# Attention with normalised q and k, then a squared-ReLU feed-forward: fewer rows of rounding beside the attention, q's transposes moved, loads in three groups

## The chip, the cores and the metric

The kernel runs on one core of a Trainium2 chip. The metric is the device time of one execution in microseconds, as the median of several runs. One further execution was recorded by the hardware profiler; all lines of profile below come from it. The engines of a core are TensorE (PE; its weight loads are listed as PEld), VectorE (DVE), ScalarE (ACT), GpSimd (POOL) and SyncE (SP), which here only issues DMAs. Each works through its own queue in order and waits on semaphores for the others.

## The reference

Eight batches of twelve heads, 448 tokens, head size 64; then a feed-forward layer over 3584 tokens with 768 inputs and 2048 hidden units.

```python
def rmsnorm(x, g):
    rms = np.sqrt(np.mean(x * x, axis=-1, keepdims=True) + 1e-06)
    return x / rms * g
q_n, k_n = rmsnorm(q, g_q), rmsnorm(k, g_k)
scores = np.matmul(q_n, k_n.transpose(0, 1, 3, 2)) / np.sqrt(64)
attn = softmax(scores)
x = np.matmul(attn, v).transpose(0, 2, 1, 3).reshape(3584, 768)
h = np.maximum(x @ w_in, 0.0)
out = (h * h) @ w_out
```

q, k, v and the gains are float32; the weights w_in and w_out come as float64 and are brought to float32 in the kernel, word by word. That is "the rounding".

## The kernel before

All is float32. Two heads make a pair (128 rows of q, k and v transposed), six pairs a batch, two batches a span, four spans. The kernel's order is written out by hand: Python generators yield between steps, and a loop puts the steps of two of them beside each other.

The first attention (`attention_alone`, pairs 0 to 11, NAT = 12) stands alone, with the rounding of w_in beside it. Then comes L1 of span 0 (`first_product(work, 0)`), the first product with w_in, with the rest of the rounding beside it; then, for each next span, its attention beside the second product of the span before, and so on. The products use seven block products for eight (A11, S2, S1, S3, A12, A22, S4), and the combined weight blocks are written to DRAM (`w1s`, `w2s`) by the rounding and read back as `sw`.

One pair i of the first attention takes four steps, each ended by a yield:

- Step 1: scores (i,0) and (i,1) on TensorE (L812), their exponentials on ScalarE (L816); k's four transposes for pair i+1 (L787) into a PSUM bank, copied to `qkT` by ScalarE (L789); the last eight products of the values of pair i-1 (L875); VectorE adds up probabilities (L829); the square and the sums for the norm of pair i+2 (L727 to L729).
- Step 2: q's four transposes for pair i+1 (L787) into the same bank as k's, copied with the gain by ScalarE (L791); v of the next pair is loaded; `roots(i + 2)` takes the inverse root through a logarithm and an exponential on ScalarE (L738, L739), three small operations on VectorE (L740 to L742), and GpSimd multiplies q by it (L743). Pairs 1 and 2 do this in `normalise_in_turn` instead, with a power on GpSimd (L336) and the product on VectorE (L339).
- Step 3: scores (i,2) and (i,3); the totals of pair i-1 (L900), of two parts for odd pairs and three for even ones; the first eight products of the values of pair i; then `finish(i - 1)` on VectorE: two transposes and a reciprocal of the totals (L918 to L920) and the product L924, which reads the values' bank.
- Step 4: VectorE adds up further (L829) and combines x (L934 to L939).

PSUM banks: scores use two buffers of two banks (`ps_s`); the values of even pairs lie in bank "o", those of odd pairs in bank "n", the totals in "t"; the transposes of steps 1 and 2 in bank "m".

The rounding (`prepare`, one row of weights after another, 32 rows: 16 of w_in, 16 of w_out) takes four ticks a row. A row costs ScalarE an absolute value (L594) and a copy of the low words (L611), VectorE a clamp (L608), a shift (L613) and a mask (L618), and one sum: for rows before EARLY/4 in two halves on GpSimd (L580), for later ones on VectorE (L584). Each two rows make four combinations on GpSimd (L588) and one write of 1344 KB to DRAM (L603). The row's words, 768 KB, are loaded four rows ahead (L545, L548). `weights(upto)` runs the ticks up to a number that grows with the step u: in the attention up to EARLY, in L1 of span 0 from EARLY to ALL = 140 over its 56 units.

L1 has HF = 8 groups of seven units. A unit u multiplies one weight block (192 KB) by three chunks (L1100). The block's buffer is one of five, so block u+4 is issued in unit u (L677) once unit u-1 is through. SyncE's queue holds all of these in order: the blocks, the words of the rounding, its writes, which wait for GpSimd, and, at unit 40, v for pair 12 (L713, L715) and q and k for pair 14 (L696) of the next attention.

Of the kernel before, what the change touches and what calls it, by code (L numbers as in the profile page):

```python
# [10 lines left out]
F32 = mybir.dt.float32  # L11
U32 = mybir.dt.uint32
AF = mybir.ActivationFunctionType
# [298 lines left out]
def load_q(nc, qk, q, i):  # L312

    _, H, S, D = q.shape
    b, h0 = divmod(2 * i, H)
    nc.sync.dma_start(places_of(qk, i, 0)[:S // 4, 0].rearrange("p (h e) -> p h e", h=2),
                      q[b, h0:h0 + 2].rearrange("h (p j) d -> p h (j d)", j=4))


def load_k(nc, qk, k, i):  # L320

    _, H, S, D = k.shape
    b, h0 = divmod(2 * i, H)
    dst = places_of(qk, i, 0)[:S // 4, 1].rearrange("p (j h d) -> p j h d", j=4, h=2)
    for h in range(2):
        nc.sync.dma_start(dst[:, :, h], k[b, h0 + h].rearrange("(p j) d -> p j d", j=4))
# [18 lines left out]
def chunk_of(pt, s, j, n):  # L345

    return pt.rearrange("d (j p) -> d j p", j=n)[:, j] if s else pt.rearrange("d (p j) -> d j p", j=n)[:, j]
# [45 lines left out]
def attention_then_ffn_bounded(  # L393
# [35 lines left out]
    nc = tc.nc  # L429

    B, H, S, D = q.shape
    NT, DM = out.shape
    DFF = w_in.shape[1]
    P = 128
# [3 lines left out]
    NFC = DFF // P  # L438
# [9 lines left out]
    NAT = 2 * NPAIR  # L448
# [12 lines left out]
    ps_o = ctx.enter_context(tc.tile_pool(name="ps_o", bufs=1, space=bass.MemoryType.PSUM))  # L461
# [3 lines left out]
    def bank(name, n=None):  # L465

        turn[0] += n is None
        return ps_m.tile([P, S], F32, tag="mn"[turn[0] % 2 if n is None else n], name=name)

    qk, qkT, ident, mhalf, gains, rstd0, _ = held  # L470
# [20 lines left out]
    HW = HC * P  # L491
    WORDS, BLOCKS, EXPS = 7, 2, 4

    EARLY, ALL = 4 * 12, 4 * (2 * NFC + 3)
    assert DM == NW and BLOCKS * 8 * HW + EXPS * NW + 2 * NW <= 3 * HF * S and 2 * NW <= 4 * S and HF % 4 == 0


# [156 lines left out]
    N1 = HF * 7  # L654
# [25 lines left out]

    pts = {}
    vs, probs, pavs, tots, normed, rstds = {}, {}, {}, {}, {}, {0: rstd0}
    places, halves, rests = [], [], {}
    sums = {"out": [dram.tile([2 * S // 32, 32], F32, name=f"factors{n}") for n in range(2)]}

    def load(i):
        if i < NAT:
            load_q(nc, qk, q, i)
            load_k(nc, qk, k, i)
            return  # L690

        b, h0 = i // NPAIR, 2 * (i % NPAIR)
        for s, src in enumerate((q, k)):
            dst = by_squares(i, 0)[:, s]
            for n in range(4):
                nc.sync.dma_start(dst[n * 32:(n + 1) * 32],  # L696
                                  src[b, h0 + n // 2, :, n % 2 * 32:n % 2 * 32 + 32]
                                  .rearrange("(g t) e -> t g e", t=32))

    def by_squares(i, work):  # L700
        n = i % 2 * 4 + 2 * work
        flat = qk[:, n:n + 2].rearrange("p n e -> p (n e)")[:, 0:2 * S]
        return flat.rearrange("p (s g e) -> p s g e", s=2, e=32)
# [78 lines left out]

    def transpose(i, s, n):

        pt = bank("pt", n)
        for j in range(NJ):
            nc.tensor.transpose(chunk_of(pt, s, j, NJ), normed[i][s][:, j * P:(j + 1) * P], ident[:SP, :SP])  # L787
        if s:
            nc.scalar.copy(qkT[:, i % 2, s], pt)  # L789
        else:  # L790
            nc.scalar.activation(qkT[:, i % 2, s], pt, AF.Copy, scale=gains[:, 0:1])  # L791

    def scores(i, c):

# [73 lines left out]
    def values(i, chunks=range(NJ)):  # L868
        if 0 in chunks:
            pavs[i] = ps_o.tile([P, S], F32, tag="o", name="pav") if i >= NAT or i % 2 == 0 else bank("pav", 1)  # L870
        if i >= NAT:
            return later_values(i)
        for c in chunks:
            for h in range(2):
                nc.tensor.matmul(pavs[i][h * D:(h + 1) * D, :], vs[i][:SP, h, c, :], probs[i, c][:, h, :],  # L875
                                 start=(c == 0), stop=(c == NJ - 1))
# [12 lines left out]
    def added(i):  # L889

        return 3 if i % 2 and i + 1 < NAT else 2
# [16 lines left out]
    def finish(i):  # L908

        b, hp = divmod(i, NPAIR)  # L910
        x = factors = xT[:, b % 2, hp]
        if i < NAT:
            pav = pavs.pop(i)


            turned, factors = sums["turned"], sums["factors"]
            few = small.tile([P, S // 32], F32, tag="few", name="few", bufs=1)
            nc.vector.transpose(turned, tots.pop(i))  # L918
            nc.vector.reciprocal(few, turned.rearrange("p (g r) -> p g r", r=32)[:, :, 0])
            nc.vector.transpose(factors.rearrange("p (g r) -> p g r", r=32),  # L920
                                few.rearrange("p g -> p g ()").to_broadcast([P, S // 32, 32]))
        else:
            pav = rests.pop(i)
        nc.vector.tensor_tensor(x, pav, factors, ALU.mult)  # L924
        del vs[i]
# [15 lines left out]
    def attention_alone():  # L941


        for i in range(NAT):
            more = i + 1 < NAT
            if 0 < i < NAT - 3:
                load(i + 3)
            scores(i, 0)
            scores(i, 1)
            if i == 0:  # L950

                transpose(1, 1, 1)
                scores(0, 2)
                scores(0, 3)
                transpose(1, 0, 0)
                add_up(0, 1)
                norm(2)
                load_v(1)
                values(0, (0, 1))
                load(3)  # L960
                yield
                continue
            if more:
                transpose(i + 1, 1, 0)
            values(i - 1, (2, 3))
            add_up(i, 1)
            if i + 2 < NAT:
                norm(i + 2)
            elif not more:
                norm(NAT)  # L970
            yield
            if more:
                transpose(i + 1, 0, 0)
            if more:
                load_v(i + 1)
            if i + 2 < NAT:
                roots(i + 2)
            yield
            scores(i, 2)
            scores(i, 3)  # L980
            total_of(i - 1)
            values(i, (0, 1))
            finish(i - 1)
            yield
            if added(i) == 3:
                add_up(i, 2)
            combine_x(i - 1)
            if NAT <= i + 3 < NAT + 2:
                load(i + 3)
            yield  # L990
        values(i, (2, 3))
        total_of(i)
        finish(i)
        combine_x(i)

# [486 lines left out]
    with tc.tile_pool(name="words", bufs=2) as spare["pool"]:  # L1482
        load(2)
        for _ in range(2):
            load_w(loaded[0])
            loaded[0] += 1
        norm(1)
        with tc.tile_pool(name="first", bufs=2, reuse_waits="tile") as work:

            free = [gT[:, f] for f in range(NFC) if f % HF < HF - 2]  # L1490
            places[:] = [g.rearrange("p (h q) -> p h q", h=2) for g in free[:2 * NJ]]
            sums[0], sums[1] = (g.rearrange("p (h q) -> p h q", h=2) for g in free[2 * NJ:2 * NJ + 2])
            sums["turned"], sums["factors"] = (g[:, 0:S] for g in free[2 * NJ + 2:2 * NJ + 4])
            sums["ones"] = work.tile([SP, D], F32, tag="ones", name="ones", bufs=1)
            nc.vector.memset(sums["ones"], 1.0)
            sums["rebias"] = work.tile([SP, 1], F32, tag="rebias", name="rebias", bufs=1)
            nc.vector.memset(sums["rebias"], -31.5 * math.log(2.0))
            for u, _ in enumerate(attention_alone()):

                weights(min(EARLY, 2 * u + 1, 4 + (EARLY - 4) * u // (4 * NAT - 7)))  # L1500
                if u == 4 * NAT - 9:
                    load_blocks(5)
        with tc.tile_pool(name="first_product", bufs=2, reuse_waits="tile") as work:
            for u, _ in enumerate(first_product(work, 0)):
                if u == 6:

                    left = ps_s.tile([P, 2, 512], F32, tag="s", name="bits")
                    banks["bits"] = left.rearrange("p a b -> p (a b)")[:, 0:NW].bitcast(U32)
                weights(min(ALL, EARLY + (ALL - EARLY) * (u - 1) // (N1 - 6)))
                if u == 5 * N1 // 7:  # L1510
                    load_v(NAT)
                    load(NAT + 2)
                if u == N1 - 5:
                    norm(NAT + 1)
                if u == N1 - 4:
                    transposes(NAT)
                    squares(NAT + 2)
# [124 lines left out]
```

## Time and profile before

| | us |
|---|---|
| runs | 1339.31, 1340.26, 1340.64 |
| median | 1340.26 |
| profiled execution | 1340.13 |
| its span | 1338.3 |
| first attention, in the span | 8.9 to 128.3 |
| L1 of span 0, in the span | 128.3 to 257.4 |
| TensorE busy | 1322.2 |

In the table of waits, "A <- B: us, times, longest" says that engine and line A waited for B. In a timeline a row has its start, its length, engine and line, what is written and read, the number of instructions, and in brackets the idle time before it and what ended it. One matrix product of float32 shows as two instructions of TensorE, so three products of a unit are six rows. In the table by stretches each engine has its busy time, and the last columns are the granted clock of TensorE, the busy share of the DMA engines and GB/s.

The groups of VectorE between 140 and 240 us, with busy time and mean length of one in ns, show what the rounding costs there:

```profile
L613 DVE TENSOR_SCALAR bits<-gC 128x768 uint32<-128x768 uint32 x18 | 17.2, 957 | 0.4
L608 DVE TENSOR_SCALAR gC<-gC 128x768 f32<-128x768 f32 x19 | 15.5, 817 | 1.0 <-ACT gC L594 1.0
L584 DVE CUSTOM_DVE_ANT_0 gC<-words,gC 128x1536 uint16<-128x1536 uint16 x10 | 11.0, 1097 | 0.0
L618 DVE SCALAR_TENSOR_TENSOR gC<-words,bits 128x768 uint32<-128x768 uint32 x9 | 8.6, 952 | 0.2
```

### The profile page before, as it was taken

The numbers are of one execution on the slowest core, as the hardware profiler recorded it, in microseconds if no ns is written. First come the engines' busy times: TensorE is split into PE (matmuls) and PEld (weight loads), VectorE is DVE, ScalarE is ACT, GpSimd is POOL, SyncE is SP. The second block draws the span as 40 slices with busy tenths as digits, with TensorE's granted clock in tenths as the row PEclk, the third lists the DMA queues.
The fourth block names the chain that finished last, engine by engine and source line by source line (L and its number), as shares of the span: only waits on it lengthen the run. The fifth ranks groups of instructions, "written<-read, shape, count | busy, mean of one in ns | idle before, by whom it ended". The sixth has DMA issues, their size and how long they took to land.

```text
span 1338.3 us, 17760 instructions
## 1 busy us (share of the span) xinstructions
PE 1322.2 (99%) x5930; PEld 698.8 (52%) x5930; DVE 857.3 (64%) x1334; ACT 486.5 (36%) x939; POOL 681.2 (51%) x544
## 2 busy tenths in 40 slices
PE   8999999999999999999999999999999999999997
PEld 3333454444446655444444855544444665556887
DVE  6998898489988233467887523457878723336553
ACT  7885656554540012245443011235554101111000
POOL 5677434376756222657774522448666522322452
PEclk9999999999999999999999999999999999999999
DMA  8786999657664332356666433345664444421333
GB/s 226 223 216 189 354 382 318 198 119 137 135 152 123 87 85 87 102 120 126 136 133 149 99 96 87 92 114 115 135 129 126 109 101 140 132 87 50 115 102 59
DMA packets 413817, 190.18 MB, mean 142 GB/s; under 512 B 282388, under 2 KB 408724, under 8 KB 413716
## 3 DMA queue, kind: packets, MB, share of 16 engines
q1 hardware_dynamic: 406164, 180.21, 51.3%
q0 software_dynamic: 4736, 8.40, 2.5%
q8 instruction: 49, 0.80, 0.3%
q10 hardware_dynamic: 2816, 0.34, 0.2%
q14 instruction: 52, 0.43, 0.1%
HBM read 155.72 MB, written 33.16 MB: 141 GB/s over the span
## 4 chain that ended last, share of the span: by engine, by line
PE 91%; DVE 3%; ACT 3%; DMA 1%; issue 1%; POOL 0%; SPq 0%; ACTq 0%; DVEq 0%
PE ps L1200 21%; PE pd L1100 10%; PE pa L1100 10%; PE pc L1100 10%; PE sc L804 7%; PE pav L886 7%; PE pb L1100 5%; PE ps L1383 3%; PE ps L1251 2%; PE pd L1355 2%; PE pc L1355 2%; PE pa L1355 2%; PE sc L812 1%; PE pd L1185 1%; PE tot L900 1%; PE pc L1185 1%
## 5 line engine op out<-in xcount | busy, mean ns | idle before, releaser
L1072 POOL TENSOR_TENSOR gT<-gT 128x448 f32<-128x448 f32 x96 | 93.9, 980 | 258.3 <-ACT gT L1068 258.3
L769 POOL TENSOR_TENSOR half<-half,mhalf 128x28 f32<-128x28 f32 x36 | 184.9, 5136 | 68.2 <-DVE half L768 51.7
L1200 PE MATMUL ps<-gT,sw 128*128 128x448 f32 x432 | 169.3, 545 | 0.0
L1068 ACT ACTIVATE gT<-gT 128x448 f32<-128x448 f32 x96 | 55.3, 576 | 295.8 <-DVE gT L1116 295.6
L1100 PE MATMUL pa<-xT,sw 128*128 128x448 f32 x384 | 154.9, 539 | 1.5 <-DMA sw<-w1s 1.5
L1200 PEld LDWEIGHTS ps<-gT,sw 128*128 128x128 f32 x432 | 80.1, 190 | 87.2 <-issue 84.8
L1200 PE MATMUL ps<-gC,sw 128*128 128x448 f32 x288 | 113.1, 546 | 0.0
L1100 PEld LDWEIGHTS pa<-xT,sw 128*128 128x128 f32 x384 | 72.8, 190 | 72.4 <-issue 72.4
L804 PE MATMUL sc<-qkT 64*64 64x448 f32 (+1 forms) x1152 | 110.0, 496 | 0.3 <-ACT pr L806 0.2
L588 POOL TENSOR_TENSOR gC<-gC 128x384 f32<-128x384 f32 x64 | 71.6, 1136 | 62.4 <-DVE gC L584 60.7
L854 POOL DMA_DIRECT2D xT<-factors x72 | 38.1, 534 | 90.9 <-DMA factors<-square 62.1
L1200 PEld LDWEIGHTS ps<-gC,sw 128*128 128x128 f32 x288 | 53.2, 190 | 59.5 <-issue 57.9
L1116 DVE TENSOR_TENSOR gT<-z,pd 128x448 f32<-128x448 f32 x32 | 19.9, 621 | 100.1 <-PE pd L1100 100.0
L806 ACT ACTIVATE pr<-sc 128x896 f32<-128x896 f32 x87 | 77.0, 909 | 12.1 <-PE sc L804 12.0
L771 POOL TENSOR_TENSOR qk<-qk,half 128x448 f32<-128x448 f32 x72 | 77.5, 1096 | 2.8
L1100 PE MATMUL pc<-xC,sw 128*128 128x448 f32 x192 | 77.5, 540 | 0.5 <-DMA sw<-w1s 0.5
L1100 PE MATMUL pd<-xT,sw 128*128 128x448 f32 x192 | 77.8, 541 | 0.2
L1100 PE MATMUL pd<-xC,sw 128*128 128x448 f32 x192 | 77.5, 540 | 0.0
L1100 PE MATMUL pc<-xT,sw 128*128 128x448 f32 x192 | 77.4, 539 | 0.0
L1100 PE MATMUL pb<-xC,sw 128*128 128x448 f32 x192 | 77.4, 539 | 0.0
L886 PE MATMUL pav<-pr,vt 64*64 64x448 f32 x348 | 72.7, 537 | 0.0
L886 PE MATMUL rest<-pr,vt 64*64 64x448 f32 x348 | 72.7, 537 | 0.0
(282 smaller groups left out, 2451.2 us busy)
## 6 DMA issues: line engine op xcount, KB each, us to landing
sw<-w1s SPq DMA_DIRECT2D x224, 192.0 KB, 2.4
sw<-w2s SPq DMA_DIRECT2D x102, 256.0 KB, 3.5
w1s<-gC SPq DMA_DIRECT2D x8, 1344.0 KB, 6.6
w2s<-gC SPq DMA_DIRECT2D x8, 1344.0 KB, 6.9
qk<-in_q_dram SPq DMA_DIRECT2D x144, 56.0 KB, 2.4
qk<-in_k_dram SPq DMA_DIRECT2D x144, 56.0 KB, 2.3
xT<-factors POOLq DMA_DIRECT2D x72, 112.0 KB, 3.4
words<-in_moe_w_out_dram SPq DMA_DIRECT2D x9, 768.0 KB, 7.5
```

The lines of the kernel that those rows point to most:

```text
L588: nc.gpsimd.tensor_tensor(*[blocks_of(n)[:, place_of(n, i)] for i in (dst, x, y)], op)
L769: nc.gpsimd.tensor_tensor(half, half, mhalf, ALU.pow)
L771: nc.gpsimd.tensor_tensor(qkn[:, s], raw[:, s], half[:, s * NG:(s + 1) * NG].rearrange("p g -> p g ()").to_broadcast([P, NG, 32]), ALU.mult)
L804: nc.tensor.matmul(sc[part, h, 0:n], qkT[rows, 0, 1, keys], qkT[rows, 0, 0, of], start=True, stop=True)
L806: nc.scalar.activation(pr, sc[:, :, 0:n], AF.Exp)
L886: nc.tensor.matmul(into, vs[i][rows, h, c, :], probs[i, c][rows, h, :], start=(c == 0), stop=(c == NF), skip_group_check=True)
L1068: nc.scalar.activation(g, src, AF.Relu)
L1072: nc.gpsimd.tensor_tensor(g, g, g, ALU.mult)
L1100: nc.tensor.matmul(ps, stream[n + at][:, c], rhs[:, c], start=first and c == 0, stop=c == HC - 1, skip_group_check=not first)
L1200: nc.tensor.matmul(ps, stream[n][:, c % 4], rhs_of[i][:, c], start=c == 0, stop=c == HF - 1)
L1355: nc.tensor.matmul(ps, lhs[:, c], rhs[:, c], start=first and c == 0, stop=c == HK - 1, skip_group_check=not first)
L1383: nc.tensor.matmul(ps, weights_of(o, m, c // HK)[:, c % HK], rhs_of[i][:, c, part], start=c == 0, stop=c == HF - 1)
```

## The change

Three edits.

1. EARLY is 4 * 11 for 4 * 12. Eleven rows are rounded beside the first attention, twenty-one beside L1. The twelfth row's sum moves from GpSimd to VectorE with it, as do its words' place in the order and the ticks' pace.
2. In the first attention, q's transposes for pair i+1 stand directly after k's, in step 1, and no longer in step 2. They go to a bank of their own: "n" for even pairs, "o" for odd ones, that is the bank in which the values of pair i-1 do not lie, and which those of pair i take in step 3. The copy with the gain stays in step 2 on ScalarE. Pair 1, in the steps of pair 0, stays as it was.
3. The loads at unit 40 of L1 are three groups: q of pair 14 after unit 40, k after unit 44, v of pair 12 after unit 48 (N1 = 56). Before, v came first.

A variable in `finish` is renamed to make room for the name `turned`.

```diff
-    EARLY, ALL = 4 * 12, 4 * (2 * NFC + 3)
+    EARLY, ALL = 4 * 11, 4 * (2 * NFC + 3)
...
+        load_part(i, 0)
+        load_part(i, 1)
+
+    def load_part(i, s):
+
         b, h0 = i // NPAIR, 2 * (i % NPAIR)
-        for s, src in enumerate((q, k)):
-            dst = by_squares(i, 0)[:, s]
-            for n in range(4):
-                nc.sync.dma_start(dst[n * 32:(n + 1) * 32],
-                                  src[b, h0 + n // 2, :, n % 2 * 32:n % 2 * 32 + 32]
-                                  .rearrange("(g t) e -> t g e", t=32))
+        dst = by_squares(i, 0)[:, s]
+        for n in range(4):
+            nc.sync.dma_start(dst[n * 32:(n + 1) * 32],
+                              (q, k)[s][b, h0 + n // 2, :, n % 2 * 32:n % 2 * 32 + 32]
+                              .rearrange("(g t) e -> t g e", t=32))
...
     def transpose(i, s, n):
 
-        pt = bank("pt", n)
+        if n is None:
+            pt = bank("pt", 1) if i % 2 == 0 else ps_o.tile([P, S], F32, tag="o", name="pt")
+        else:
+            pt = bank("pt", n)
         for j in range(NJ):
             nc.tensor.transpose(chunk_of(pt, s, j, NJ), normed[i][s][:, j * P:(j + 1) * P], ident[:SP, :SP])
         if s:
             nc.scalar.copy(qkT[:, i % 2, s], pt)
+        elif n is None:
+            turned[i] = pt
         else:
-            nc.scalar.activation(qkT[:, i % 2, s], pt, AF.Copy, scale=gains[:, 0:1])
+            gain(i, pt)
+
+    def gain(i, pt):
+        nc.scalar.activation(qkT[:, i % 2, 0], pt, AF.Copy, scale=gains[:, 0:1])
...
             if more:
                 transpose(i + 1, 1, 0)
+                transpose(i + 1, 0, None)
             values(i - 1, (2, 3))
...
             yield
             if more:
-                transpose(i + 1, 0, 0)
+                gain(i + 1, turned.pop(i + 1))
...
-                if u == 5 * N1 // 7:
+                if u in (N1 - 16, N1 - 12):
+                    load_part(NAT + 2, (u - N1 + 16) // 4)
+                if u == N1 - 8:
                     load_v(NAT)
-                    load(NAT + 2)
```

More of the change, by code (lines that the diff above doesn't have):

```diff
@@ L682, in attention_then_ffn_bounded @@
     vs, probs, pavs, tots, normed, rstds = {}, {}, {}, {}, {}, {0: rstd0}
-    places, halves, rests = [], [], {}
+    places, halves, rests, turned = [], [], {}, {}
     sums = {"out": [dram.tile([2 * S // 32, 32], F32, name=f"factors{n}") for n in range(2)]}
@@ L913, in finish @@
             pav = pavs.pop(i)
-            turned, factors = sums["turned"], sums["factors"]
+            flat, factors = sums["turned"], sums["factors"]
             few = small.tile([P, S // 32], F32, tag="few", name="few", bufs=1)
-            nc.vector.transpose(turned, tots.pop(i))
-            nc.vector.reciprocal(few, turned.rearrange("p (g r) -> p g r", r=32)[:, :, 0])
+            nc.vector.transpose(flat, tots.pop(i))
+            nc.vector.reciprocal(few, flat.rearrange("p (g r) -> p g r", r=32)[:, :, 0])
             nc.vector.transpose(factors.rearrange("p (g r) -> p g r", r=32),
```

## The prediction

> **What bounds the kernel now.** I read the page first (busy time, chain), then the waits of TensorE alone, split at the end of the first attention, then the timeline of each engine around those waits.
>
> ```profile
> span 1338.3 us, 17760 instructions
> PE 1322.2 (99%) x5930; PEld 698.8 (52%) x5930; DVE 857.3 (64%) x1334; ACT 486.5 (36%) x939; POOL 681.2 (51%) x544
> PE 91%; DVE 3%; ACT 3%; DMA 1%; issue 1%; POOL 0%; SPq 0%; ACTq 0%; DVEq 0%
> ```
>
> TensorE is busy 99% of the span. The change takes no matrix product away, so only the 16 us in which TensorE stands still can be won, and 7.6 us of these are the tail after 1320 us, which the change doesn't touch. The rest, by TensorE's waits (us in total, times, longest), first from 8 to 125 us, then from 125 us on:
>
> ```profile
> PE pt L787 <- ACT qkT L789: 2.0, 5, 1.0
> PE sc L812 <- ACT qkT L389: 0.8, 1, 0.8
> PE sc L812 <- ACT gT L816: 0.6, 1, 0.6
> ...
> PE pa L1100 <- DMA sw<-w1s: 1.5, 1, 1.5
> PE pc L1100 <- DMA sw<-w1s: 0.5, 1, 0.5
> ```
>
> The first line is what the second edit is about (q's transposes wait until ScalarE has copied k's out of the bank), the last two what the third is about. The two waits on weight blocks are longer from start to start: a unit of L1 (one block, three products) starts 2.255 us after the last one, but the units at 212.67 and 234.75 came 2.90 and 3.94 us after theirs, so they cost 0.65 and 1.68, together 2.3 us. In the attention I compare each pair's length with an undisturbed one (10.01 us where the totals take three parts, 9.26 where two): from the starts of L812's first scores, pairs 1, 2, 5, 8, 9, 10 are late by 0.40, 1.17, 0.56, 0.69, 0.55, 0.32, with 0.05 at pair 4 a sum of 3.7 us. So 6 us is the ceiling, 0.45% of the time.
>
> **What the skill says.** The Trainium skill, "PSUM — Partial Sum Buffer", section "PSUM bank collisions raise a hardware error", has it that two engines must not be on one bank at once, so a bank is guarded as a whole. That is why the second group of transposes must wait for the copy in one bank, and why in the new place it waits for whoever read that bank last. The 2.0 us above agree. "DMA: Bandwidth & Descriptors", section "Specifications", asks for at least 512 B a transfer for full rate; q's and k's pieces here are 128 B, and the stretch 220 to 230 us falls to 169 GB/s while they run, though there the issue (0.5 us each) also limits. "Issuing engines are not separate DMA queues" of that page says all DMAs end on the same 16 engines; the landings agree, a block of 192 KB issued behind a row and a write lands after 7 us, alone after 2.35.
>
> **The second edit, step by step.** Instructions on TensorE and ScalarE stay the same in number: eight transposes a pair (0.53 us per four) and two copies. Only q's four move ahead of the eight products of the values (1.65 us), into a second bank. The wait on L789 goes, 2.0 us plus 0.1 of refill. But moving earlier makes three other releases count.
>
> (a) q must be normalised. From pair 3 on GpSimd's product (L743) ends 1.7 us or more ahead of the new place (the transposes at 48.5, in pair 4's steps, need the one that ended at 45.4). For pair 2, transposed in pair 1's steps, VectorE does it late (L339); TensorE's timeline, then VectorE's (start, us, instruction, wait before it):
>
> ```profile
> 17.14 0.60 PE L787 MATMUL pt<-ident,qk 112*128 112x112 f32 x4
> ...
> 19.72 0.60 PE L787 MATMUL pt<-ident,qk 112*128 112x112 f32 x4 [0.33 <-ACT qkT L789]
> ...
> 30.93 0.57 PE L787 MATMUL pt<-ident,qk 112*128 112x112 f32 x4 [1.03 <-ACT qkT L789]
> ```
>
> ```profile
> 18.52 0.69 DVE L339 TENSOR_TENSOR qk<-qk,rstd 112x512 f32<-112x512 f32 x1 [1.75 <-POOL rstd L336]
> ...
> 58.08 0.62 DVE L924 TENSOR_TENSOR xT<-pav,gT 128x448 f32<-128x448 f32 x1
> ```
>
> The new place is 17.67, q is there at 19.21: 1.55 us of a new wait, with the values and everything after queued behind it on TensorE. Scores (1,2) start at 19.26+0.53+1.65 = 21.44, not 20.25: 1.2 late. In pair 2 the 1.03 wait and what hangs on it are gone, and I get scores (2,2) at 31.46 against 31.44. So pairs 1 and 2 together: nothing, half of the 2.0 us.
>
> (b) The bank must be read out by the product L924 of two pairs back. It ends 27.7, 37.2, 47.2, 58.7, 67.3, 76.8, 86.3, 96.4, 106.8 us; the new place is at the pair's first scores plus 2.23: 28.1, 38.5, 48.5, 57.8 to 58.1, 68.4, 77.7, 87.7, 97.9, 108.2. Only pair 5 is late, 0.4 to 0.6 for the 0.22 won there.
>
> (c) Where ScalarE's exponentials (L816) hold the next scores, as at pairs 8 and 9, a wait removed from the transposes is only taken later. Pair 10's 0.23 is real.
>
> **The first edit in the attention.** One row less in 40 steps: ScalarE 0.92+0.93, VectorE 0.55+0.55+0.95, GpSimd two sums of 1.0. All lie beside TensorE. They count where ScalarE's Ln waits for VectorE (L729) and the exponentials queue behind. From pair 2 on each pair now has one row exactly, with its absolute value (L594, 0.92) behind the square and no longer between the logarithm and the exponentials, where pairs 8 and 9 have it. Against that, VectorE has the mask (L618, 0.95) ahead of the next norm. For pairs 5, 8, 9 I take 0.3, 0.2, 0.5 us of their 0.56, 0.69, 0.55, less 0.3 for (b). With pair 10 that is 0.9 us for the attention; bounds +0.5 (bank late at more pairs) and -2.2.
>
> **The first edit in L1.** One row more: VectorE four operations (0.82, 0.96, 0.95, 1.1, 3.8 us). It runs 0.48 rows a unit for 0.46 (96 and 92 ticks over 50 units, four a row), so VectorE rises from 36.0 of 40 us to about 93%. No release of it holds TensorE now, and I cost it nothing; gone wrong, some 0.3 us at a few units, 1 us. The DMAs are the tighter place:
>
> ```profile
> 140.00:180.00 40.00, 40.00 (x107) 20.06 (x106) 37.29 (x46) 26.08 (x41) 14.88 (x15) 1.00 1.00 365
> 180.00:220.00 40.00, 39.52 (x106) 19.76 (x105) 36.04 (x45) 24.16 (x37) 16.68 (x17) 1.00 1.03 387
> 220.00:230.00 10.00, 10.00 (x28) 5.04 (x27) 9.07 (x12) 7.97 (x13) 4.75 (x5) 1.00 0.73 169
> ```
>
> (The last three columns are TensorE's clock, the DMA engines' busy share and GB/s.) A unit asks for 196.6 KB of block and, a row, 786.4 KB read and 688.1 written: 196.6+0.46*1474.5 = 875 KB before, 388 GB/s, which is what was delivered; after it 904 KB, 401 GB/s. Stretches of 8 us reached 403 and 410, so 387 is what was asked, no limit shown. At 403 the new demand fits; at 387 a unit takes 2.337, and over the 33 units from the first row to the last the blocks come 2.7 us late. I take 395: 2.290, 1.15 us late. Blocks have 0.6 to 0.8 us to spare at the worst units (the one issued at 165.25 landed 7.74 later, 0.7 before its unit); a row and a write now fall into one unit more often, so I let this spare go.
>
> **The third edit.** The queue of SyncE:
>
> ```profile
> 215.22 4.83 SPq L677 DMA_DIRECT2D sw<-w1s  x3
> 220.10 1.56 SPq L713 DMA_DIRECT2D vt<-in_v_dram  x2
> 221.70 1.33 SPq L715 DMA_DIRECT2D vt<-in_v_dram  x2
> 223.08 2.16 SPq L696 DMA_DIRECT2D qk<-in_q_dram  x4
> 225.28 2.04 SPq L696 DMA_DIRECT2D qk<-in_k_dram  x4
> 227.42 0.43 SPq L677 DMA_DIRECT2D sw<-w1s  x1
> ```
>
> Twelve issues take 7.3 us; the next block, free to go at 221.8, goes at 227.42, and the one after stands behind a write of 1344 KB. In three groups the longest block of issues is 2.1 to 2.9 us, of which a unit hides 1.8. The 1.68 goes. k now comes at unit 44 and v at 48, still 8 units ahead of the square of pair 14 and of the next attention: 18 us against a landing of 2 to 4. Other things queued on SyncE (the writes at units 42, 46, 50) already wait for GpSimd.
>
> L1: 0.65 that stays plus 1.15 is 1.8 for 2.3, a gain of 0.5; bounds -2.3 and +2.9.
>
> **Sum.** 1340.13 of the profiled execution (span 1338.3 and 1.8 around it) minus 0.9 minus 0.5 is 1338.7. The median of the runs is 1340.26, 0.13 above; I forecast 1338.8. About 0.2%, 2.7 us, is what can be told from no change here.
>
> **Rivals.** A, likeliest (0.52): as above, 1338.8, by itself 1337.3 to 1340.4. B (0.27): both waits go nearly whole. ScalarE and VectorE, each lighter by a row, are early, so the attention keeps only the 1.6 at pair 1 (-2.1), and L1 keeps a short wait (-1.9): 1336.2. For it, the DMA's 410 GB/s; against it, the chain in pairs 1 and 2 already runs over ScalarE. C, slower (0.12): the DMA engines fall behind in L1. At 378 GB/s (what 158 to 166 us showed) a unit takes 2.393, 4.5 late over 33 units, stalls 5.2 for 2.3: with an attention that wins nothing 1343.1. It decides below 388 GB/s, where it eats the attention's 0.9. Against it, 387 was demand. D (0.09): the moved transposes do not do what they are for, the wait only passes from L789 to L339 and L924, and L1 stays as it is: 1340.3.
>
> Faster by over 0.2% (below 1337.6): 0.25 of B, 0.05 of A, 0.30. Slower (above 1342.9): 0.09. Within: 0.61. Range 1335.9 to 1342.2: half of B's spread below is left out, and half of C.
>
> **What would show it.** TensorE's waits in the attention should name DVE (L339's product at pair 1, about 1.5 us; the L924 product once) and no longer the copy of k; the start of L1 should come at 127.4 for 128.28. In L1 no wait of over 1 us after 225 us, several of 0.1 to 0.6 on blocks between 160 and 225 us, DMA at 390 to 400 GB/s from 180 to 220 us. Wrong would be: waits on blocks of over 3 us in sum (C), none at all (B), or an unchanged start of L1 (D).

## The result: slower by 0.2 to 0.3%, and where the profile after puts it

The changed kernel takes 1343.79 us as a median of nine runs (1342.25 to 1345.80), the kernel before 1340.26 beside it (1338.33 to 1340.98): 3.5 us between the medians. The estimate of the ratio is 1.0022, with a 95% interval of 1.0012 to 1.0032. Run again on another occasion it took 1344.35, ratio 1.0030 (1.0017 to 1.0042). The forecast was 1338.8 with a range up to 1342.2: the time went the other way.

The line numbers move in the changed kernel: the transposes are L794, k's copy L796, the gain L803, scores L824, exponentials L828, sums of probabilities L841, the norm L731 to L733, logarithm and exponential L742 and L743, the product that frees the bank L936, L1 L1113. The profiled execution has a span of 1343.0. TensorE's waits from 8 to 125 us, then from 125 us on (A <- B: us, times, longest):

```profile
PE sc L824 <- ACT gT L828: 3.6, 3, 2.1
PE pt L794 <- ACT gT L828: 1.6, 1, 1.6
PE sc L824 <- ACT qkT L389: 0.8, 1, 0.8
...
PE pav L887 <- ACT gT L828: 1.0, 1, 1.0
PE pd L1198 <- DVE pr L1280: 1.0, 2, 0.6
PE pa L1113 <- DMA sw<-w1s: 0.8, 1, 0.8
```

The two lines that the change aimed at did what they should: no wait for k's copy, and of the waits for weight blocks one of 0.8. In their place stand 3.6 us in which the scores, and 1.0 in which the values, wait for ScalarE's exponentials, and 1.6 at q's transposes in pair 1. This last one is the wait on q's norm that was forecast, though the table names an exponential: in all seven profiles with pair 2's q moved, these transposes start 0.145 to 0.147 us after q's product (L339) ended, but 0.10 to 0.12 after the exponential, so the product is the steady one. The length of each pair's steps, from the start of its first scores on TensorE to that of the next pair's (of pair 11, to L1), sums the loss up; the last two columns are L1 from its first to its last product, and the start of L1:

| kernel | pair 0 | 1 | 2 | 3 | 4 | 5 | 6 | 7 | 8 | 9 | 10 | 11 | L1 | L1 starts |
|---|---|---|---|---|---|---|---|---|---|---|---|---|---|---|
| before | 6.53 | 10.41 | 10.43 | 10.01 | 9.31 | 10.57 | 9.26 | 10.01 | 9.94 | 10.56 | 9.58 | 12.74 | 128.72 | 128.28 |
| changed | 7.74 | 11.70 | 9.11 | 9.86 | 9.48 | 10.16 | 10.43 | 10.16 | 11.23 | 10.34 | 9.41 | 14.76 | 127.62 | 133.32 |
| changed, again (e11) | 6.53 | 11.67 | 9.11 | 9.86 | 9.49 | 10.16 | 10.45 | 10.16 | 10.35 | 10.33 | 9.41 | 14.77 | 128.14 | 131.14 |

L1 is 0.6 to 1.1 us shorter. The attention is 2.9 to 3.8 us longer, once the start is set aside: pair 0's 7.74 is a lower granted clock in the first 20 us, which the same program did not have the second time. Pairs 6, 8 and 11 carry the loss; what pair 1 loses, pair 2 gives back. What follows L1 took 1080.8 us before and 1081.5 and 1082.2 after. The other profiles lie between 1081.1 and 1083.3 there, so the 0.7 to 1.4 us that are longer there can't be put down to the change; where they come from stays open. Pair 8, in the changed kernel's timeline, first VectorE, then ScalarE, then TensorE (start, length, instruction, idle time before it and its releaser):

```profile
88.77 0.62 DVE L936 TENSOR_TENSOR xT<-pav,gT 128x448 f32<-128x448 f32 x1
89.31 1.42 DVE L613 TENSOR_SCALAR gC<-gC 128x768 uint32<-128x768 uint32 x1
90.65 1.90 DVE L841 TENSOR_TENSOR gT<-gT 112x896 f32<-112x896 f32 x1
92.48 0.61 DVE L946 TENSOR_TENSOR xC<-xT 128x448 f32<-128x448 f32 x1
93.01 0.94 DVE L618 SCALAR_TENSOR_TENSOR gC<-gC 128x768 uint32<-128x768 uint32 x1
93.88 1.91 DVE L841 TENSOR_TENSOR gT<-gT 112x896 f32<-112x896 f32 x1
95.71 1.21 DVE L732 TENSOR_REDUCE rstd<-qk 112x16 f32<-112x1024 f32 x1
96.95 0.17 DVE L733 TENSOR_SCALAR rstd<-rstd 112x16 f32<-112x16 f32 x1
```

```profile
93.13 0.69 ACT L803 ACTIVATE qkT<-pt,gains 128x448 f32<-128x448 f32 x1
97.16 0.22 ACT L742 ACTIVATE half<-rstd 112x16 f32<-112x16 f32 x1 [3.34 <-DVE rstd L733]
97.41 0.31 ACT L743 ACTIVATE half<-half,rebias 112x16 f32<-112x16 f32 x1
97.62 1.66 ACT L828 ACTIVATE gT<-sc,rstd 112x448 f32<-112x448 f32 x3
```

```profile
95.09 1.67 PE L887 MATMUL pav<-gT,vt 112*64 112x448 f32 x8
98.82 1.68 PE L824 MATMUL sc<-qkT 64*112 64x448 f32 x6 [2.05 <-ACT gT L828]
```

In these rows VectorE never idles. Between the product that finishes pair 6 (L936; VectorE is that far behind) and the norm of pair 10 (L732, L733) stand two operations of the rounding, the shift (L613) and the mask (L618). The norm is ready 8.35 us after L936 began; ScalarE waits 3.34 us for it, its exponentials stand behind the logarithm, and TensorE waits 2.05 us for a score buffer before pair 9's first scores.

In the second profile of the same program pair 8 took 10.35 us and this last wait 1.17. The order on VectorE was the same, but the shift was short:

```profile
88.02 0.55 DVE L613 TENSOR_SCALAR gC<-gC 128x768 uint32<-128x768 uint32 x1
```

That is 0.55 us for 1.42, and the difference is about the 0.88 between the two pairs. So in these two profiles the size of the loss at pair 8 varies; that pairs 6, 8 and 11 lose does not.

### The profile page after: what moved, and what is told of

The parts are those of the page before. It is cut to its first block, busy times and chain, and to the rows that moved or that the text cites. A ratio compares the mean times of both kernels' runs of the same rounds, so it can differ in the third digit from the quotient of the medians.

```text
span 1343.0 us, 17773 instructions
## 1 busy us (share of the span) xinstructions
PE 1322.9 (99%) x5930; PEld 699.4 (52%) x5930; DVE 865.1 (64%) x1335; ACT 486.2 (36%) x939; POOL 671.1 (50%) x542
## 4 chain that ended last, share of the span: by engine, by line
PE 87%; DVE 7%; DMA 2%; ACT 2%; issue 1%; POOL 0%; SPq 0%; DVEq 0%; POOLq 0%; ACTq 0%
PE ps L1213 21%; PE pd L1113 10%; PE pa L1113 10%; PE pc L1113 10%; PE sc L816 7%; PE pav L898 7%; PE pb L1113 5%; PE ps L1396 3%; PE ps L1264 2%; PE pd L1368 2%; PE pa L1368 2%; PE pc L1368 2%; DMA sw<-w1s 1%; PE pd L1198 1%; PE pc L1198 1%
## 5 line engine op out<-in xcount | busy, mean ns | idle before, releaser
L1113 PE MATMUL pa<-xT,sw 128*128 128x448 f32 x384 | 155.0, 540 | 0.8 <-DMA sw<-w1s 0.8
L1113 PEld LDWEIGHTS pa<-xT,sw 128*128 128x128 f32 x384 | 72.8, 190 | 71.7 <-issue 70.2
L1113 PE MATMUL pd<-xT,sw 128*128 128x448 f32 x192 | 77.9, 542 | 0.2
L1113 PE MATMUL pc<-xT,sw 128*128 128x448 f32 x192 | 77.5, 540 | 0.0
L1113 PE MATMUL pc<-xC,sw 128*128 128x448 f32 x192 | 77.4, 539 | 0.0
L1113 PE MATMUL pb<-xC,sw 128*128 128x448 f32 x192 | 77.4, 539 | 0.0
L1113 PE MATMUL pd<-xC,sw 128*128 128x448 f32 x192 | 77.4, 539 | 0.0
```

The lines of the kernel that those rows point to most:

```text
L1113: nc.tensor.matmul(ps, stream[n + at][:, c], rhs[:, c], start=first and c == 0, stop=c == HC - 1, skip_group_check=not first)
```

## The experiments

Theory P (phase): what costs is where in a pair's four steps the ticks of the rounding fall on VectorE, not how many rows there are. With eleven rows the pace is one row a pair, so from pair 2 on every pair has the same order: absolute value, clamp, shift, mask in steps 1 to 4, and the last two lie ahead of the next norm. With twelve rows the order drifts: in the trace of the kernel before, the mask alone stands ahead of the norm in pairs 3 and 4, the clamp alone in pairs 5 to 7, clamp and shift in pairs 8 and 9, and shift and mask together in none. Theory M (move): the moved transposes make the wait. Theory C: the slow start is all there is. Each kernel was timed against the kernel before, in five rounds.

**e1_rows_only, e2_move_only, e3_split_only, e4_move_split_12rows: the edits apart.**

```diff
# e1: the kernel before, and only
-    EARLY, ALL = 4 * 12, 4 * (2 * NFC + 3)
+    EARLY, ALL = 4 * 11, 4 * (2 * NFC + 3)
# e4: the changed kernel with 4 * 12; e2: e4 with the loads at unit 40 as before;
# e3: e4 with transpose(i + 1, 0, 0) in step 2 as before
```

> The kernel before with eleven rows beside the first attention, nothing else of the change. Theory P (phase): with eleven rows every pair has the same ticks, the shift and the mask of a row lie on VectorE between the finish of one pair and the norm of the next, ScalarE's logarithm waits for VectorE (14.9 us in sum after, 9.9 before) and the exponentials behind it hold TensorE. Then this edit alone makes the attention 3 to 4 us longer (start of L1 at 131 to 132.5, with TensorE waiting for exponentials at pairs 6, 8, 11), and L1 1 to 2 us longer or equal, 1343 to 1346 in all. Theory M (the moved transposes make the wait): the attention is as before, start of L1 at 127.5 to 129, 1340 to 1342. Theory C (the slow start, clock 0.88 between 10 and 20 us, is chance): nothing of either beyond 1.3 us of the start.

> q's transposes moved, twelve rows and the loads as before. P: the wait for k's copy is gone, 1.6 us of wait come at pair 1, the rest of the attention as before or shorter: start of L1 at 127 to 129, total 1339 to 1341. M: start of L1 at 131 to 132.5, total 1343 to 1344.

> The loads in three groups, all else as before. Both theories: the wait of 1.5 us for a block near 234 us is gone, the small one near 212 stays, the attention is as before: 1338 to 1339. If the loads only push a wait elsewhere: 1340.

> All of the change but the row: twelve rows, transposes moved, loads in groups. P: 1337.5 to 1339.5, faster than before. M: 1341.5 to 1343.

| | median us | ratio to before, interval | L1 starts | L1 |
|---|---|---|---|---|
| e1, rows | 1344.70 | 1.0034 (1.0021 to 1.0048) | 131.37 | 128.99 |
| e2, move | 1342.16 | 1.0011 (1.0004 to 1.0018) | 129.33 | 128.50 |
| e3, loads | 1339.27 | 0.9990 (0.9982 to 0.9997) | 127.96 | 126.95 |
| e4, move and loads | 1340.67 | 1.0003 (0.9995 to 1.0012) | 129.70 | 127.12 |

The rows alone cost as much as the whole change; the two intervals overlap. In e1's table of TensorE's waits from 8 to 125 us the transposes stand where they stood, and the exponentials hold the scores all the same:

```profile
PE sc L812 <- ACT gT L816: 2.7, 3, 1.5
PE pt L787 <- ACT qkT L789: 1.1, 5, 0.3
```

Pairs 4, 6, 8 and 11 take 9.87, 10.05, 10.81 and 14.39 us, and pair 0 takes 6.52. That ends C, and M as the main cause. The move alone was above what P allowed (1339 to 1341) and below what M asked: it costs 0.1%, and L1 starts 1.05 us later than before. In e2's timeline of TensorE one wait of it is the bank:

```profile
58.33 0.61 PE L794 MATMUL pt<-ident,qk 112*128 112x112 f32 x4
59.57 0.57 PE L794 MATMUL pt<-ident,qk 112*128 112x112 f32 x4 [0.64 <-DVE xT L936]
```

The others, at pairs 4 and 8 (9.78 and 10.53 us), are exponentials again. The loads in groups gain, and in L1: 1.77 us; their 1339.27 is just above the range of 1338 to 1339. e4, the move and the loads together, fell between the two theories (P up to 1339.5, M from 1341.5): it is as fast as the kernel before, because what the loads gain in L1 the move loses in the attention.

**e5_phase_shifted and e9_phase_by_one: the phase alone.**

```diff
# e5: the changed kernel, and only
-weights(min(EARLY, 2 * u + 1, 4 + (EARLY - 4) * u // (4 * NAT - 7)))
+weights(min(EARLY, 2 * u + 1, 6 + (EARLY - 4) * u // (4 * NAT - 7)))
# e9: 5 + for 6 +
```

> The changed kernel with all three edits, eleven rows too, but the ticks of the rounding two steps earlier from pair 2 on: the shift falls into step 1, the mask into step 2, the absolute value into step 3, the clamp into step 4. The work of every engine is the same. P: the norm of the next pair comes in time, TensorE no longer waits for exponentials at pairs 6, 8 and 11; start of L1 at 128 to 129.5, total 1338 to 1340.5. If the number of rows or the new place of the transposes is the cause and not the phase: 1343 to 1344.5 as the changed kernel.

> The changed kernel with the ticks one step earlier: clamp in step 1, shift in step 2, mask in step 3, absolute value in step 4. P: only the mask lies on VectorE between a finish and the next norm, the wait at pairs 6 and 8 falls by half or more; start of L1 at 126 to 129, total 1338 to 1341. If only the very place of e5 helps: 1343.

e5 takes 1337.14 us, ratio 0.9976 (0.9967 to 0.9984): all three edits and the same work, with one number changed, and faster than both kernels; it is also faster than P said (1338 to 1340.5, start of L1 at 128 to 129.5). L1 starts at 125.40. Pairs 4 to 10 take 9.11 and 9.86 us in turn, with nothing lost, and pair 11 takes 12.70. Some 2 us of the gain are this last pair, in which no rounding is left, as its ticks came two steps earlier. In e5 TensorE's waits from 8 to 125 us are two, and neither is of the kind that the changed kernel had at pairs 6 and 8 (the first is pair 1's, on q's norm):

```profile
PE pt L794 <- ACT gT L828: 1.6, 1, 1.6
PE sc L824 <- ACT qkT L389: 0.8, 1, 0.8
```

ScalarE's waits for the norm, in the kernel before (8 to 130 us), in the changed kernel and in e5 (8 to 135 us):

```profile
ACT half L738 <- DVE rstd L729: 9.9, 9, 2.3
```

```profile
ACT half L742 <- DVE rstd L733: 14.9, 9, 3.3
```

```profile
ACT half L742 <- DVE rstd L733: 3.9, 9, 1.1
```

And pair 8 of e5 on VectorE, to set beside the eight lines above:

```profile
84.87 0.62 DVE L936 TENSOR_TENSOR xT<-pav,gT 128x448 f32<-128x448 f32 x1
85.41 1.30 DVE L841 TENSOR_TENSOR gT<-gT 112x896 f32<-112x896 f32 x1
86.64 0.61 DVE L946 TENSOR_TENSOR xC<-xT 128x448 f32<-128x448 f32 x1
87.17 0.55 DVE L608 TENSOR_SCALAR gC<-gC 128x768 f32<-128x768 f32 x1
87.92 1.63 DVE L841 TENSOR_TENSOR gT<-gT 112x896 f32<-112x896 f32 x1 [0.19 <-ACT gT L828]
89.47 1.21 DVE L732 TENSOR_REDUCE rstd<-qk 112x16 f32<-112x1024 f32 x1
90.71 0.17 DVE L733 TENSOR_SCALAR rstd<-rstd 112x16 f32<-112x16 f32 x1
90.80 0.55 DVE L613 TENSOR_SCALAR gC<-gC 128x768 uint32<-128x768 uint32 x1
```

Of the rounding only the clamp (0.55) is left ahead of the norm, VectorE even idles 0.19 there, and shift and mask come after it. From L936 to the norm it is 6.0 us for 8.35. The kernel before had the same order in pairs 5 to 7, by its drift, and pairs 6 and 7 lost nothing there (9.26 and 10.01). Its pair 6:

```profile
68.80 0.55 DVE L608 TENSOR_SCALAR gC<-gC 128x768 f32<-128x768 f32 x1
...
72.34 0.17 DVE L729 TENSOR_SCALAR rstd<-rstd 112x16 f32<-112x16 f32 x1
72.42 0.55 DVE L613 TENSOR_SCALAR gC<-gC 128x768 uint32<-128x768 uint32 x1
```

The chain of the work that ended last agrees. In the changed kernel, from 8 to 133 us, the sums of probabilities are 11.5% of it, the mask 5.7% and the shift 4.8%; in e5, from 8 to 130 us, it runs over TensorE almost alone.

e9 takes 1341.14 us, 1.0006 (0.9997 to 1.0014), just above its range, and in its finer form the theory fails: the wait of the logarithm is 14.5 us, no less than in the two profiles of the changed kernel (14.9 and 13.3), and TensorE's wait for exponentials 2.5 (3.6 and 2.7), with pairs 6 and 8 at 9.76 and 10.52. What e9 does gain over the changed kernel lies in pair 11 (13.33 for 14.77) and pair 6. The mask is then the only operation ahead of the norm, but it lasts longer, and ScalarE now has the copy of the low words (L611) between the logarithm's exponential and the scores'. VectorE of pair 8, then ScalarE:

```profile
88.09 1.72 DVE L618 SCALAR_TENSOR_TENSOR gC<-gC 128x768 uint32<-128x768 uint32 x1
89.73 1.91 DVE L841 TENSOR_TENSOR gT<-gT 112x896 f32<-112x896 f32 x1
```

```profile
95.62 0.31 ACT L743 ACTIVATE half<-half,rebias 112x16 f32<-112x16 f32 x1
95.83 0.89 ACT L611 ACTIVATE gT<-gT 128x768 int32<-128x768 uint32 x1
96.62 2.18 ACT L828 ACTIVATE gT<-sc,rstd 112x448 f32<-112x448 f32 x4
```

So counting the operations ahead of the norm is not enough. The phase also moves the rounding's work on ScalarE and GpSimd, and no run moves that on one engine alone: that the phase is the cause is shown, how its cost divides among the three engines is not.

**e6_rows_phase_no_move: does the phase help without the other edits?** e1 with the same edit as e5.

> Eleven rows as in e1_rows_only, with the ticks two steps earlier, transposes and loads as before. P: the 4 us that e1_rows_only lost are gone without the other edits; pairs run at their undisturbed 10.0 and 9.3 us, start of L1 at 126.5 to 128, total 1338.5 to 1340.5. If the shift of the ticks helps only together with the moved transposes: 1342 to 1344.

1338.77 us, 0.9990 (0.9981 to 0.9998), 5.9 us below e1. Pairs 3 to 10 take 10.01 and 9.26 us, L1 starts at 125.66, a little earlier than forecast, and the wait of the logarithm is 3.9 us for 16.3 in e1. The phase needs neither the move nor the loads.

**e7_12rows_steady, e8_12rows_pair2_late, e10_11rows_pair2_late: towards a better version.** e7 is e4 with e5's phase and pace, so that the twelfth row falls into pair 11. e8 and e10 leave pair 2's q where it was:

```diff
# e7 against e4
-4 + (EARLY - 4) * u // (4 * NAT - 7)
+6 + (EARLY - 8) * u // (4 * NAT - 7)
# e8 against e7, e10 against e5
-                transpose(i + 1, 0, None)
+                if i > 1:
+                    transpose(i + 1, 0, None)
...
-            if more:
+            if more and i > 1:
                 gain(i + 1, turned.pop(i + 1))
+            elif more:
+                transpose(i + 1, 0, 0)
```

> Transposes moved, loads in groups, the ticks two steps earlier at one row a pair as in e5_phase_shifted, but running on to twelve rows in the last pair. P: the attention ends as in e5 (125.4) or up to 0.5 later, L1 with one row less is 0.5 shorter, total 1336 to 1337.5. If the number of rows beside the attention is itself a cost: start of L1 1 to 2 us later, 1338 to 1339.5.

> As e7_12rows_steady, with q's transposes for pair 2 (in pair 1's steps) left in step 2 and k's bank, where they wait for k's copy and not for q's norm. Pair 1 takes 10.4 us for 11.7, pair 2 stays at 9.1 to 9.4 if its length in before came from its own wait for k's copy: total 1.0 to 1.3 below e7. If ScalarE holds pair 2 (as the chain of before has it), pair 2 takes 10.2 and the total is e7's.

> e5_phase_shifted (eleven rows, all three edits, ticks two steps earlier) with q's transposes for pair 2 left in step 2 as in e8. P: pair 1 takes 10.4 us for 11.7 and pair 2 9.4 to 10.1, pair 11 stays at 12.7 (13.8 in e8, with its twelfth row), L1 at 127.6: total 0.3 to 1.2 below e5, about e8's. If ScalarE takes the gain back in pair 2 whole, e5's time.

e7 takes 1337.83 (0.9979, 0.9970 to 0.9987), e8 1336.89 (0.9972, 0.9964 to 0.9980), e10 1336.62 (0.9976, 0.9967 to 0.9986). e7 is 0.3 us above its range and e8 0.9 us below e7, a little less than forecast; e7's profile has the slow pair 0. The twelfth row costs 1.1 us in pair 11 (13.81 for 12.70) and gives 1.2 back in L1 (126.40 for 127.64): with the phase set, the number of rows is a draw. Pair 2's q left in step 2 takes pair 1 from 11.7 to 10.4 us, and pairs 1 and 2 together from 20.78 (e5) to 19.65 (e10); pairs 3 and 11 give 0.6 of this back, in this one profile each. By the intervals e5, e7, e8 and e10 can't be told apart. They are the fastest, some 2.8 to 3.9 us under the kernel before.

**e11_after_again.** The changed kernel unchanged.

> The changed kernel itself once more, on the same chip as e10. The slow start (1.2 us, clock 0.88 between 10 and 20 us in its profile) is chance if pair 0 takes 6.5 us here; the waits of pairs 6, 8 and 11 on exponentials come again: 1342.5 to 1344.5. If the slow start is a mark of this program, pair 0 takes 7.7 us again.

Pair 0 takes 6.53 us; the pairs are in the table above. The slow start was no mark of the program, and the waits at pairs 6, 8 and 11 come again, that of pair 8 smaller.

## Why the prediction was wrong

- The loads in groups: right. The 1.68 us was to go; L1 alone with this edit is 1.77 shorter.
- One row more in L1: right in sum, not in place. Waits for blocks were put at 1.8 us in all; a unit of 2.255 us makes 125.9 for what the table calls L1, so before lost 2.8 and after 1.7 (2.2 the second time). But the prediction had its lateness ahead of 225 us and nothing left after the loads; in the trace 0.93 of the 1.7 falls on the one unit that starts at 229.64. The row's own price was put at 1.15; between profiles that differ in the row it is 0.3 (e1 and before) to 1.3 (e10 and e8). The DMA engines were to deliver 390 to 400 GB/s from 180 to 220 us, and VectorE to be busy at about 93%. By stretches (the busy times of the engines, clock, DMA share, GB/s):

```profile
180.00:220.00 40.00, 39.95 (x106) 19.79 (x106) 38.31 (x47) 26.68 (x41) 18.71 (x19) 1.00 1.04 398
```

  That is 398, and 96% for VectorE, without a wait of TensorE for it. Rival C named nearly the right time, 1343.1, but its mechanism, DMA engines that fall behind in L1, didn't occur: the nearness is luck.
- The moved transposes: the waits were right, the sum was not. The wait at pair 1 was put at 1.55 us and is 1.65, and pairs 1 and 2 together at nothing, 20.81 for 20.84. The late bank at pair 5 was put at 0.4 to 0.6 and is 0.64 in e2; in the changed kernel the product had freed the bank 0.26 us before. But the move alone (e2) starts L1 1.05 us later, with 0.47 lost at pair 4 and 0.59 at pair 8. The prediction put nothing at pair 4 and, at pair 8, a wait that is only taken later. With the phase set, the move's own worth is small: L1 starts at 125.40 in e5 and at 125.66 in e6, in one profile each. The rule on banks that the prediction cites is not tested here: k's and q's transposes of a pair write the same 448 columns, so the second four have to wait for the copy in any case.
- The step that failed is "The first edit in the attention", where one row less was to give pairs 5, 8 and 9 back 0.3, 0.2 and 0.5 us; with the rest of its terms the attention came to -0.9, and to +0.5 at worst. Alone (e1) the edit makes the attention 3.1 us longer; with the phase moved as well (e6) L1 starts 2.6 us earlier than before. The prediction had the new order of the ticks and named the mask ahead of the next norm, but set it off against the absolute value that no longer stands ahead of the exponentials, in three pairs, with the lengths of before. It left out that the shift comes with the mask in every pair, where the kernel before had at most clamp and shift there, and that sums of 1.1 us last 1.9 in this place and the shift up to 1.4. The wait of the logarithm for the norm rose from 9.9 us to 14.9 and 13.3.
- "One row less" was also the wrong name for the edit. Its weight was in the pace: EARLY is the slope of the tick schedule.

## What to carry to other kernels

When a generator's work is spread over the steps of another loop, the number that sets how much is done also sets where each piece falls; write out which operations then stand ahead of the critical one on each in-order engine, for several turns in a row, before pricing the amount. A pace of exactly one unit a turn makes one order permanent, a good one or a bad one, so choose its phase: here two ticks were worth some 6 us, more than the three edits together. An engine without idle time ahead of a short operation that another engine waits for is the place to look at.

## What the runs showed of the hardware

- Eight transposes in a row take less than twice four: L794 eight at a time took 0.91 us from start to the next product, four and four apart 1.06. So an undisturbed pair is 9.11 and 9.86 us long after the move for 9.26 and 10.01. This was not in the prediction.
- Some operations of VectorE stretch while GpSimd adds. The sum of probabilities (L841), with two inputs, takes 1.09 us alone and up to 1.91 beside GpSimd's two sums of the rounding, which themselves take 4.56 us there for 2.00 alone. The shift (L613), with one, takes 0.55 alone and 1.42 in pair 8 of the changed kernel. The Trainium skill, "GPSIMD Engine Reference", section "1. Specifications", says that GpSimd's SBUF interfaces are shared with VectorE, with contention where VectorE has two SBUF inputs or is in a 2-port performance mode. For the sums these traces agree; whether the shift is in such a mode no run shows. In pair 8 the two sums take 3.81 us in the changed kernel and 2.93 in e5, and the shift 0.87 more than alone, so stretching makes, as an estimate, about 1.7 of the 2.35 us between the two norms. How much of the phase's cost it makes in all was not tried by itself.
- The granted clock of TensorE was 0.88 between 10 and 20 us in the profile of the changed kernel and 1.00 in its second one. Seen closer, it was 0.50 from 9.0 to 12.4 us and 1.00 after that; it cost 1.2 us of pair 0. Three of the thirteen profiles show such a pair 0 (7.74 us), in three different programs.
